# Block-diagonal head product of a linear attention block as three one-pass products of parts

## The chip, the core and the metric

The kernel runs on one core of one Trainium2 chip. The metric is device time in microseconds (us), the median of several executions. Its engines are named as the profile names them: PE is TensorE's matmul, PEld its weight load, DVE VectorE, ACT ScalarE, POOL GpSimd, SP SyncE, which issues nearly all DMAs. Each engine works through its own queue in order; an instruction that waits holds up all that stands behind it on its engine.

## The reference

A linear attention block without softmax, then a two-layer feed-forward block with the gate `h * erf(softplus(h))`:

```python
# q, k, v: (batch 8, heads 8, seq 576, head_dim 64), g_norm: (64,)
kv = np.einsum('bhsd,bhse->bhde', k, v)
out = np.einsum('bhsd,bhde->bhse', q, kv)
rms = np.sqrt(np.mean(out * out, axis=-1, keepdims=True) + 1e-06)
attn = out / rms * g_norm
x = attn.transpose(0, 2, 1, 3).reshape(4608, 512)
h = x @ w_in                                   # (4608, 2048)
sp = np.maximum(h, 0.0) + np.log1p(np.exp(-np.abs(h)))
g = h * erf(sp)
result = g @ w_out                             # (4608, 512)
```

All inputs of the attention are float32; the weights come as float64.

## The kernel before

**Tiles.** The tokens are cut into nine groups of 512: group T = 0 to 7 holds the first 512 positions of batch T, group 8 the last 64 positions of all eight batches. The heads go in pairs, p = 0 to 3. For a pair, two 64x64 products of k and v stand on the diagonal of a 128x128 matrix `bd`; one matmul with `bd` as weights applies both heads to the 128x512 transposed q (line 325, "the product" below). The last 64 positions of the pair go through a small matmul of their own (line 324, the "tail"), and are kept in `x_last` for group 8.

**Number formats.** A matmul on float32 operands is two instructions in the trace; on `float32r` operands it is one. The large products of the later groups are made of float32r parts. `thirds` (line 424) cuts a tensor into `high` (a rounded copy, ACT), `low` (the rest, DVE) and `both` (4096 low + high, DVE); `lower_w` (line 431) does the like for weights. `product` (line 449) then adds up high*high and low*low in the bank `n_ps` and both*both in the bank `m_ps`, and the result is `4095 n_ps + m_ps`: ACT or DVE scales `n_ps` into SBUF, and DVE adds `m_ps` (`add`, line 444).

**Phases.** Groups 0 and 1 and the first attention pairs are worked off by 250 us, with the weights converted, cut into parts and written to DRAM. From there to the end a loop over periods m = 8 to 36 (from line 787) runs groups 2 to 8 and reads the parts of the weights back from DRAM by SP. A period makes four *units* (tiles of 128 columns of h) of a group's first layer, and four *results* (rows of 128 tokens) of the second layer for the four units of the period before; b = m mod 4 is the number of the period within its group. In a period the order in which instructions are issued is, for each of the four units i: 12 matmuls (`hidden`, line 506); for i = 0 ACT's `cut_upper` of both halves of the gated h of the period before; for i = 0 and 1 DVE's `cut_lower` of one half (two 128x1024 operations); ACT's scaling of `n_ps` and DVE's `add` of `m_ps` into h; ACT's softplus. Then two Erf operations on ACT. Then for each of the four results j: 12 matmuls (`result`, line 766), DVE's scaling of `n_ps` (for b = 1, where the sum of a group starts, as a `tensor_scalar` into `es[j]`, line 776; else `add_scaled`), and DVE's `add`. After result 1 DVE multiplies h by the gate (line 876). The matmul products turn through six PSUM banks in pairs.

**The pieces of the attention.** In group T's period b the pair p = b of group T+1 is prepared, as six pieces that `attention` returns: products with loads of later pairs, apply, halve, mean, norm, split. The tuple `places` (line 800) says where each is put: place 0 is ahead of unit 0, place i+1 behind unit i, place 5+j behind result j. So before the change, `products` (k*v, the transposes of q, DVE's copies to `bd`, ACT's copy of `qT`) stands ahead of unit 0, `apply` (tail, product, the copy to `x_last`, ACT's square) behind unit 1, `halve` (DVE splits the squares into two float32r parts) and the loads behind unit 2, `mean` (matmul with a matrix of means, and Ln, Exp and Square on ACT between two table loads) behind result 0, `norm` (three DVE operations) behind result 1, `split` (`thirds` of x) behind result 3. In a group's last period (b = 3) split comes one place earlier.

**Banks and buffers of the attention.** `ps_at` has two banks, for `kv_ps`, `qt_ps`, `se_ps` and `ms_ps` in turn. SBUF tiles with one buffer each carry the tags `qT`, `rms_r`, `sq_lo` and, in pool `x_new`, `x`.

Of the kernel before, what the change touches and what calls it, by code (L numbers as in the profile page):

```python
# [39 lines left out]
FP32 = mybir.dt.float32  # L40
# [14 lines left out]
FIRST = 2  # L55
# [5 lines left out]
def kernel(  # L61
# [207 lines left out]
    def attention(T, p, pools=None):  # L269

        st = {}

        halves = FIRST <= T < B
        bd = bd_kv[:, (T * NP + p) % 2, :]

        q_tail, o_tail = slice(P, 2 * P), slice(2 * P, 2 * P + R)

        def bank(name):
            pool, tag = (pools or {}).get(name, (ps_at, "at"))
            return pool.tile([P, G], FP32, name=name, tag=tag)  # L280

        def square_tile(name):

            if T == 0:
                return gate.tile([P, G], FP32, name=name, tag="h")
            return attp.tile([P, G], FP32, name=name, tag="qT")

        def products():

            kv_ps = st["kv"] = bank("kv_ps")  # L290
            ks, vs, qs = (x.pop((T, p)) for x in (k_sb, v_sb, q_sb))
            C = chunks(T)
            for c in range(C):
                rows = slice(0, S // C + (c < S % C))
                for i in range(2):
                    s = slice(i * D, i * D + D)
                    nc.tensor.matmul(  # L297
                        kv_ps[s, s],
                        lhsT=ks[rows, i, c],
                        rhs=vs[rows, i, c],  # L300
                        start=(c == 0),
                        stop=(c == C - 1),
                    )
            if p % 2 == 0:
                nc.tensor.transpose(kv_ps[:, q_tail], q_last[:, p // 2], ident)
            if p == NP - 2:
                for i in range(NP):
                    load_last(T + 1, i)
            st["qT"] = square_tile("qT")
            for i in range(2):  # L310
                s = slice(i * D, i * D + D)
                nc.vector.tensor_copy(out=bd[s, s], in_=kv_ps[s, s])
            if p % 2 == 0:
                tails[T] = attp.tile([P, P], FP32, name="qT_last", tag="t")
                nc.vector.tensor_copy(out=tails[T], in_=kv_ps[:, q_tail])
            st["tail"] = tails[T][:, p % 2 * R : p % 2 * R + R]
            qt_ps = bank("qt_ps")
            for j in range(J):
                nc.tensor.transpose(qt_ps[:, j * P : j * P + P], qs[:, j], ident)  # L319
            nc.scalar.copy(st["qT"], qt_ps)  # L320

        def apply():
            qT, o_ps, kv_ps = st["qT"], bank("se_ps"), st.pop("kv")
            nc.tensor.matmul(kv_ps[:, o_tail], lhsT=bd, rhs=st.pop("tail"), start=True, stop=True)  # L324
            nc.tensor.matmul(o_ps, lhsT=bd, rhs=qT, start=True, stop=True)  # L325
            nc.vector.tensor_copy(out=x_last[:, p, T * R : T * R + R], in_=kv_ps[:, o_tail])
            st["o"] = o_ps
            nc.scalar.activation(qT, o_ps, AF.Square)

        def square():  # L330
            st["o"], st["qT"] = x_last[:, p, :], square_tile("sq")
            nc.scalar.activation(st["qT"], st["o"], AF.Square)

        def halve():
            sq = st.pop("qT")
            hi = st["hi"] = attp.tile([P, G], FP32R, name="sq_hi", tag="rms_r")
            lo = st["lo"] = attp.tile([P, G], FP32R, name="sq_lo", tag="sq_lo")
            nc.vector.tensor_copy(out=hi, in_=sq)
            nc.vector.tensor_tensor(out=lo, in0=sq, in1=hi.bitcast(FP32), op=ALU.subtract)

        def mean(table=True):
            ms = st["ms"] = bank("ms_ps")
            if halves:


                nc.tensor.matmul(ms, lhsT=mean_w, rhs=st.pop("hi"), start=True, stop=False)  # L346
                nc.tensor.matmul(ms, lhsT=mean_w, rhs=st.pop("lo"), start=False, stop=True)  # L347
                u = square_tile("u")
            else:
                u = st.pop("qT")  # L350
                nc.tensor.matmul(ms, lhsT=mean_w.bitcast(FP32), rhs=u, start=True, stop=True)  # L351
            if T > 0:
                r = attp.tile([P, G], FP32, name="rms_r", tag="rms_r")
                exp_ln_table()
            else:
                r = gate.tile([P, G], FP32, name="rms_r", tag="s")
            st["u"], st["r"] = u, r
            nc.scalar.activation(r, ms, AF.Ln, bias=eps_col)
            nc.scalar.activation(r, r, AF.Exp, scale=-0.5)
            nc.scalar.activation(u, r, AF.Square)  # L360
            if table and (T > 0 or p == NP - 1):
                softplus_table()

        def norm():
            ms, u, r = (st.pop(name) for name in ("ms", "u", "r"))
            nc.vector.scalar_tensor_tensor(
                out=u, in0=ms, scalar=EPS, in1=u, op0=ALU.add, op1=ALU.mult
            )
            nc.vector.scalar_tensor_tensor(
                out=u, in0=u, scalar=3.0, in1=r, op0=ALU.subtract, op1=ALU.mult  # L370
            )
            if T < FIRST:
                if T not in xT:
                    xT[T] = wide.tile([P, KC, G], FP32, name="xT", tag="ab"[T])
                x = xT[T][:, p, :]
            else:
                x = st["x"] = x_new.tile([P, G], FP32, name="x", tag="x")
            nc.vector.scalar_tensor_tensor(
                out=x,
                in0=st.pop("o"),  # L380
                scalar=gm_col,
                in1=u,
                op0=ALU.mult,
                op1=ALU.mult,
            )

        def split():
            if T >= FIRST:
                thirds(st.pop("x"), *(form[:, p] for form in x_forms[T]))

        def loads():
            load_pair(T * NP + p + 2)

        if T == 0:
            return products, apply, halve, mean, norm
        if T == B:
            return lambda: None, square, lambda: None, mean, norm, split

        pieces = ((products,), (apply,), (halve, loads)) if halves else ((products, loads), (apply,), ())
        return (*(partial(chain, *group) for group in pieces), mean, norm, split)  # L400

# [44 lines left out]

    banks = [(ps_h, "h"), (ps_h, "h")] + [(ps_o, f"o{i}") for i in range(4)]

    def product(weights, moving, turns=True):


        n_ps, m_ps = (
            pool.tile([P, G], FP32, name=name, tag=tag)
            for name, (pool, tag) in zip(("n_ps", "m_ps"), banks[:2])
        )
        if turns:
            banks.extend(banks[:2])
            del banks[:2]
        for ps, forms in ((n_ps, (0, 1)), (m_ps, (2,))):
            for k in range(4):  # L460
                for form in forms:
                    nc.tensor.matmul(  # L462
                        ps,
                        lhsT=weights(form, k),
                        rhs=moving(form, k),
                        start=(form == forms[0] and k == 0),
                        stop=(form == forms[-1] and k == 3),
                    )
        return n_ps, m_ps
# [276 lines left out]

    low_room.close()
    room.close()
    ctx.enter_context(tc.tile_pool(name="shift", bufs=1, side="right")).tile([P, 504], FP32, name="shift")
    late_r = ctx.enter_context(tc.tile_pool(name="late_r", bufs=1, side="right"))  # L750
    gate_r = ctx.enter_context(tc.tile_pool(name="gate_r", bufs=1, side="right"))
    w_out_p = ctx.enter_context(tc.tile_pool(name="w_out_p", bufs=7, side="right"))
# [13 lines left out]
    def result(T, b, j, g, w):  # L766

        ps = product(
            lambda form, f: g[j // 2][:, form, f, j % 2 * P : j % 2 * P + P],
            lambda form, f: w[f][:, form],  # L770
        )
        if b == 0:
            if j == 0:
                all_e = wide.tile([P, J, DM], FP32, name="e", tag="a")
                es.update((i, all_e[:, i]) for i in range(J))
            nc.vector.tensor_scalar(
                out=es[j], in0=ps[0], scalar1=SHIFT - 1.0, scalar2=None, op0=ALU.mult
            )
        else:
            add_scaled(es[j], ps[0], SHIFT - 1.0)  # L780
        add(es[j], ps[1])
# [5 lines left out]
    for m in range(first_batch, batches + 1):  # L787
# [21 lines left out]
                todo[5] = partial(chain, todo[5], softplus_table)  # L809
        elif b == NB - 1:  # L810
            places = (0, 2, 3, 5, 6, 7)

        def pieces(place):
            while todo and places[-len(todo)] <= place:
# [101 lines left out]
```

## Time and profile before

| what | value |
|---|---|
| timed runs (3) | median 944.7 us, 944.42 to 946.44 |
| span of the profiled execution | 942.4 us |
| mean granted TensorE clock | 0.999 |
| DMA over the span | 275 GB/s of HBM traffic, read and written |
| ACT table loads, all | 1283 ns each |
| first layer, n_ps matmuls | 896, mean 401 ns, 0.1 us idle before all of them |
| the product (line 325), all 32 pairs | 64 instructions, 34.9 us |

The duration of a matmul in the profile overlaps with that of the next, since they are pipelined: the distance from start to start is what a matmul takes of PE. The distance from the last event of the profile to the timed median is 944.7 - 942.4 = 2.3 us. A bracket behind a line of the timeline is the idle time of that engine ahead of the instruction, with what ended it. Busy time in four periods of the last phase, with the clock, the share of DMA and GB/s at the end of each line:

```profile
351.30:376.10 24.80, 24.80 (x133) 20.05 (x131) 20.01 (x30) 15.86 (x22) 0.00 (x0) 1.00 0.86 291
376.10:400.90 24.80, 24.80 (x136) 20.06 (x133) 20.02 (x29) 15.98 (x22) 0.00 (x0) 1.00 0.90 305
400.90:425.70 24.80, 24.80 (x134) 20.05 (x130) 20.01 (x30) 15.87 (x22) 0.00 (x0) 1.00 0.94 317
425.70:450.50 24.80, 24.80 (x136) 20.06 (x134) 19.98 (x29) 15.99 (x22) 0.00 (x0) 1.00 0.88 305
```

The columns are the stretch, its length, and the busy time of PE, PEld, DVE, ACT and POOL.

### The profile page before, as it was taken

What the parts mean: (1) busy time and instruction counts of PE and PEld (TensorE: products, weight loads), DVE (VectorE), ACT (ScalarE), POOL (GpSimd) and SP (SyncE); (2) the same over time, 40 slices, a digit from 0 to 9 for tenths busy, and PEclk for the clock granted to TensorE, in tenths of its full rate; (3) what the DMA queues carried; (4) which work ended last, traced back from release to release, by engine and by line L of the source; (5) the groups of instructions that cost most, each with busy time, mean ns of one, the idle gap of its engine ahead of it and who ended that gap; (6) DMA issues with size and microseconds to landing.
All of it is one profiled execution on the core that took longest, in us unless ns stands there. A gap on an engine that the chain in (4) does not pass through costs nothing.

```text
span 942.4 us, 11743 instructions
## 1 busy us (share of the span) xinstructions
PE 924.8 (98%) x4272; PEld 683.4 (73%) x4272; DVE 742.6 (79%) x1056; ACT 615.6 (65%) x825; POOL 2.4 (0%) x10
## 2 busy tenths in 40 slices
PE   6999999999999999999999999999999999999997
PEld 4444445666688888888888888888888888888886
DVE  3999858887577787877778888878887877787667
ACT  3899776776766666666666666666666666665551
POOL 1000000000000000000000000000000000000000
PEclk9999999999999999999999999999999999999999
DMA  9766406899699998998899889998896778778871
GB/s 257 276 204 207 150 1 227 318 351 335 214 363 335 309 325 283 306 311 307 280 287 314 294 298 309 311 303 296 293 325 260 263 253 345 284 286 287 353 263 46
DMA packets 111842, 259.78 MB, mean 276 GB/s; under 512 B 43864, under 2 KB 69544, under 8 KB 111784
## 3 DMA queue, kind: packets, MB, share of 16 engines
q1 hardware_dynamic: 110152, 256.73, 78.7%
q10 hardware_dynamic: 1568, 2.29, 0.8%
q8 instruction: 34, 0.56, 0.2%
q14 instruction: 24, 0.20, 0.1%
q0 software_dynamic: 64, 0.00, 0.0%
HBM read 224.40 MB, written 34.60 MB: 275 GB/s over the span
## 4 chain that ended last, share of the span: by engine, by line
PE 92%; DVE 4%; DMA 2%; ACT 1%; issue 0%; SPq 0%; DVEq 0%
PE n_ps L462 45%; PE m_ps L462 22%; PE o_ps L520 10%; PE h_ps L692 6%; PE se_ps L325 3%; PE kv_ps L297 2%; PE qt_ps L319 2%; DMA w_raw<-in_moe_w_in_dram 1%; PE ms_ps L351 1%; DMA v_sb<-in_v_dram 1%; DVE h L876 1%; DVE e L445 1%; PE ms_ps L346 1%; PE ms_ps L347 1%; PE kv_ps L324 1%; DVE e L440 0%
## 5 line engine op out<-in xcount | busy, mean ns | idle before, releaser
L462 PE MATMUL n_ps<-x_forms,w_in_parts 128*128 128x512 f32 x896 | 232.5, 401 | 0.1
L462 PE MATMUL n_ps<-w_out_parts,g_forms 128*128 128x512 f32 x928 | 231.2, 391 | 0.0
L462 PEld LDWEIGHTS n_ps<-w_out_parts,g_forms 128*128 128x128 f32 x928 | 174.2, 188 | 38.4 <-issue 1.4
L462 PEld LDWEIGHTS n_ps<-x_forms,w_in_parts 128*128 128x128 f32 x896 | 166.8, 188 | 43.1 <-issue 9.3
L852 ACT ACTIVATE s<-h 128x512 f32<-128x512 f32 x112 | 71.0, 633 | 178.9 <-DVE h L445 178.9
L445 DVE TENSOR_TENSOR h<-m_ps,h 128x512 f32<-128x512 f32 x116 | 79.7, 687 | 59.8 <-ACT h L837 43.8
L462 PE MATMUL m_ps<-w_out_parts,g_forms 128*128 128x512 f32 x464 | 124.2, 389 | 0.0
L462 PE MATMUL m_ps<-x_forms,w_in_parts 128*128 128x512 f32 x448 | 120.0, 390 | 0.0
L520 PE MATMUL o_ps<-w_out_sb,h_sb 128*128 128x512 f32 x224 | 100.8, 593 | 0.3 <-DVE h_sb L642 0.3
L462 PEld LDWEIGHTS m_ps<-w_out_parts,g_forms 128*128 128x128 f32 x464 | 87.1, 188 | 18.0
L462 PEld LDWEIGHTS m_ps<-x_forms,w_in_parts 128*128 128x128 f32 x448 | 84.1, 188 | 17.7
L445 DVE TENSOR_TENSOR e<-m_ps,e 128x512 f32<-128x512 f32 x116 | 80.2, 692 | 18.2 <-PE m_ps L462 10.9
L440 DVE SCALAR_TENSOR_TENSOR e<-n_ps,e 128x512 f32<-128x512 f32 x88 | 60.3, 685 | 39.2 <-PE n_ps L462 39.2
L520 PEld LDWEIGHTS o_ps<-w_out_sb,h_sb 128*128 128x128 f32 x224 | 42.3, 190 | 48.9 <-issue 46.6
L411 DVE SCALAR_TENSOR_TENSOR g_forms<-g_forms 128x1024 fp32r<-128x1024 f32 x58 | 71.1, 1225 | 2.0
L408 DVE TENSOR_TENSOR g_forms<-h,g_forms 128x1024 fp32r<-128x1024 f32 x58 | 70.6, 1217 | 1.7 <-ACT g_forms L405 1.4
L876 DVE TENSOR_TENSOR h<-h,s 128x1024 f32<-128x1024 f32 x58 | 68.3, 1218 | 0.7 <-ACT s L856 0.7
L837 ACT ACTIVATE h<-n_ps 128x512 f32<-128x512 f32 x112 | 65.5, 585 | 3.4 <-PE n_ps L462 3.4
L405 ACT ACTIVATE g_forms<-h 128x1024 fp32r<-128x1024 f32 x58 | 58.9, 1059 | 12.2 <-PE m_ps L462 8.7
L692 PE MATMUL h_ps<-xT,w_in_sb 128*128 128x512 f32 x144 | 64.9, 594 | 0.7 <-DVE w_in_sb L240 0.6
L106 ACT ACT_TABLE_LOAD x44 | 56.5, 1283 | 0.8
L856 ACT ACTIVATE s<-s 128x1024 f32<-128x1024 f32 x56 | 56.2, 1052 | 0.3
(98 smaller groups left out, 1013.3 us busy)
## 6 DMA issues: line engine op xcount, KB each, us to landing
w_out_parts<-w_out SPq DMA_DIRECT2D x116, 768.0 KB
w_in_parts<-w_in SPq DMA_DIRECT2D x112, 768.0 KB
w_in<-w_new SPq DMA_DIRECT2D x16, 768.0 KB
q_sb<-in_q_dram SPq DMA_DIRECT2D x32, 256.0 KB
w_raw<-in_moe_w_out_dram SPq DMA_DIRECT2D x8, 1024.0 KB
out_dram<-e SPq DMA_DIRECT2D x32, 256.0 KB
k_sb<-in_k_dram SPq DMA_DIRECT2D x28, 287.5 KB
v_sb<-in_v_dram SPq DMA_DIRECT2D x28, 287.5 KB
```

The lines of the kernel that those rows point to most:

```text
L106: nc.scalar.preload_act_table_set("softplus")
L405: nc.scalar.activation(high, x, AF.Copy, scale=1.0 + 2.0**-13)
L408: nc.vector.tensor_tensor(out=low, in0=x, in1=high.bitcast(FP32), op=ALU.subtract)
L411: nc.vector.scalar_tensor_tensor(out=both, in0=low.bitcast(FP32), scalar=SHIFT, in1=high.bitcast(FP32), op0=ALU.mult, op1=ALU.add,)
L440: nc.vector.scalar_tensor_tensor(out=out_, in0=ps, scalar=scale, in1=out_, op0=ALU.mult, op1=ALU.add)
L445: nc.vector.tensor_tensor(out=out_, in0=ps, in1=out_, op=ALU.add)
L462: nc.tensor.matmul(ps, lhsT=weights(form, k), rhs=moving(form, k), start=(form == forms[0] and k == 0), stop=(form == forms[-1] and k == 3),)
L520: nc.tensor.matmul(o_ps[j], lhsT=g[:, j * P : j * P + P], rhs=w_out_sb[:, f, :], start=(f == 0), stop=last,)
L692: nc.tensor.matmul(plain[i], lhsT=w_in_sb[:, c, i % FC * P : i % FC * P + P], rhs=xT[T][:, c, :], start=(c == 0), stop=(c == KC - 1),)
L837: nc.scalar.activation(h[:, i], n_ps, AF.Copy, scale=SHIFT - 1.0)
L852: nc.scalar.activation(s[:, i], h[:, i], AF.Softplus)
L876: nc.vector.tensor_tensor(out=part(h, half), in0=part(h, half), in1=part(s, half), op=ALU.mult)
```

## The change

For groups T = 3 to 7 and pairs p = 0 to 2, fifteen pairs in all (`parts` in the diff), the float32 product on `bd` becomes three float32r matmuls on parts: `kv` holds the three parts of `bd`, formed on DVE behind the copies to `bd`; `q3` holds the three parts of the transposed q, `high` taken by ACT from PSUM in place of the copy to `qT`, and `low` and `both` by DVE in a new piece, `cut`. `apply_parts` issues the tail, the three matmuls into the next pair of the six large banks, ACT's scaling of `n_ps` into `o`, DVE's add of `m_ps`, and ACT's square. Such a pair has seven pieces, at the places 0, 2, 3, 4, 6, 7, 8: products ahead of unit 0, cut behind unit 1, apply behind unit 2, halve and loads behind unit 3, mean behind result 1, norm behind result 2, split behind result 3. Some tiles take other buffers. The other pairs keep their pieces and places.

For all groups of the last phase, the scaling of the first `n_ps` of a result (b = 1) goes from DVE to ACT. A pool of 504 floats per partition that only shifted what follows gives way to one of 384 for `kv`.

```diff
@@ attention
+        parts = FIRST < T < B and p < NP - 1
@@ products
-            st["qT"] = square_tile("qT")
+            if not parts:
+                st["qT"] = square_tile("qT")
             for i in range(2):
                 s = slice(i * D, i * D + D)
                 nc.vector.tensor_copy(out=bd[s, s], in_=kv_ps[s, s])
+            if parts:
+                kv = st["kv3"] = parts_p.tile([P, 3, P], FP32R, name="kv_forms", tag="kv3")
+                nc.vector.tensor_scalar(
+                    out=kv[:, 0],
+                    in0=bd,
+                    scalar1=(1.0 + 2.0**-13) / SHIFT,
+                    scalar2=None,
+                    op0=ALU.mult,
+                )
+                lower_w(bd, *(kv[:, i] for i in range(3)))
...
-            nc.scalar.copy(st["qT"], qt_ps)
+            if parts:
+                x = st["q3"] = [
+                    pool.tile([P, G], FP32R, name=f"q_{name}", tag=tag)
+                    for name, pool, tag in (
+                        ("high", attp, "rms_r"),
+                        ("low", attp, "sq_lo"),
+                        ("both", x_new, "x"),
+                    )
+                ]
+                upper(qt_ps, x[0])
+                st["qt"] = qt_ps
+            else:
+                nc.scalar.copy(st["qT"], qt_ps)
+
+        def cut():
+            lower(st.pop("qt"), *st["q3"])
+
+        def apply_parts():
+            x, w, kv_ps = st.pop("q3"), st.pop("kv3"), st.pop("kv")
+            nc.tensor.matmul(kv_ps[:, o_tail], lhsT=bd, rhs=st.pop("tail"), start=True, stop=True)
+            n_ps, m_ps = two_banks()
+            for i, ps in enumerate((n_ps, n_ps, m_ps)):
+                nc.tensor.matmul(ps, lhsT=w[:, i], rhs=x[i], start=(i != 1), stop=(i != 0))
+            nc.vector.tensor_copy(out=x_last[:, p, T * R : T * R + R], in_=kv_ps[:, o_tail])
+            o = st["o"] = attp.tile([P, G], FP32, name="o", tag="qT")
+            nc.scalar.activation(o, n_ps, AF.Copy, scale=SHIFT - 1.0)
+            add(o, m_ps)
+            st["qT"] = x_new.tile([P, G], FP32, name="sq", tag="x")
+            nc.scalar.activation(st["qT"], o, AF.Square)
@@ mean
-                u = square_tile("u")
+                u = (
+                    x_new.tile([P, G], FP32, name="u", tag="x")
+                    if parts
+                    else square_tile("u")
+                )
@@ norm
+            elif parts:
+                x = st["x"] = u
@@ end of attention
+        if parts:
+            return products, cut, apply, partial(chain, halve, loads), mean, norm, split
@@ product: its choice of banks becomes a function, which apply_parts calls too
+    def two_banks(turns=True):
+        ps = [
+            pool.tile([P, G], FP32, name=name, tag=tag)
+            for name, (pool, tag) in zip(("n_ps", "m_ps"), banks[:2])
+        ]
         if turns:
             banks.extend(banks[:2])
             del banks[:2]
+        return ps
@@ pools of the last phase
-    ctx.enter_context(tc.tile_pool(name="shift", bufs=1, side="right")).tile([P, 504], FP32, name="shift")
+    parts_p = ctx.enter_context(tc.tile_pool(name="parts_p", bufs=1, side="right"))
@@ result
-            nc.vector.tensor_scalar(
-                out=es[j], in0=ps[0], scalar1=SHIFT - 1.0, scalar2=None, op0=ALU.mult
-            )
+            nc.scalar.activation(es[j], ps[0], AF.Copy, scale=SHIFT - 1.0)
@@ loop over periods
+        if len(todo) > len(places):
+            places = (0, 2, 3, 4, 6, 7, 8)
```

More of the change, by code (lines that the diff above doesn't have):

```diff
@@ L319, in products @@
                 nc.tensor.transpose(qt_ps[:, j * P : j * P + P], qs[:, j], ident)
-            nc.scalar.copy(st["qT"], qt_ps)
+            if parts:
[25 more added lines that the diff above has]
+            nc.scalar.activation(st["qT"], o, AF.Square)
         def apply():
+            if parts:
+                return apply_parts()
             qT, o_ps, kv_ps = st["qT"], bank("se_ps"), st.pop("kv")
@@ L397, in attention @@
             return lambda: None, square, lambda: None, mean, norm, split
+        if parts:
+            return products, cut, apply, partial(chain, halve, loads), mean, norm, split
         pieces = ((products,), (apply,), (halve, loads)) if halves else ((products, loads), (apply,), ())
@@ L447 @@
     banks = [(ps_h, "h"), (ps_h, "h")] + [(ps_o, f"o{i}") for i in range(4)]
-    def product(weights, moving, turns=True):
-        n_ps, m_ps = (
+    def two_banks(turns=True):
+        ps = [
             pool.tile([P, G], FP32, name=name, tag=tag)
             for name, (pool, tag) in zip(("n_ps", "m_ps"), banks[:2])
-        )
+        ]
         if turns:
@@ L458, in product @@
             del banks[:2]
+        return ps
+    def product(weights, moving, turns=True):
+        n_ps, m_ps = two_banks(turns)
         for ps, forms in ((n_ps, (0, 1)), (m_ps, (2,))):
@@ L775, in result @@
                 es.update((i, all_e[:, i]) for i in range(J))
-            nc.vector.tensor_scalar(
-                out=es[j], in0=ps[0], scalar1=SHIFT - 1.0, scalar2=None, op0=ALU.mult
-            )
+            nc.scalar.activation(es[j], ps[0], AF.Copy, scale=SHIFT - 1.0)
         else:
```

## The prediction

> **What bounds the kernel now.** I read the page's busy shares and chain of waits first, then the groups by form for the product that is replaced, then the timeline of PE, DVE and ACT one at a time over four periods of the last phase (one period is four units of the first layer and four results of the second, 24.78 us on average: the same PE place falls at 352.51 and, four periods on, at 451.63). Busy shares and chain:
>
> ```profile
> PE 924.8 (98%) x4272; PEld 683.4 (73%) x4272; DVE 742.6 (79%) x1056; ACT 615.6 (65%) x825; POOL 2.4 (0%) x10
> ...
> PE 92%; DVE 4%; DMA 2%; ACT 1%; issue 0%; SPq 0%; DVEq 0%
> ```
>
> PE is back to back, and the chain that ended last is PE itself. So PE time saved in a period is time gained, as long as PE never waits; and a wait put before PE costs its whole length. The average share of 79% on DVE hides the question: when in a period is DVE free? Groups by form, then PE and DVE over one period (start us, duration us, then the work):
>
> ```profile
> L325 PE MATMUL se_ps<-qT,bd_kv 128*128 128x512 f32 x64 | 34.9, 628 | 0.0
> ```
>
> ```profile
> 418.97 1.07 PE L462 MATMUL m_ps<-w_out_parts,g_forms 128*128 128x512 f32 x4
> ...
> 431.20 1.08 PE L462 MATMUL m_ps<-x_forms,w_in_parts 128*128 128x512 f32 x4
> 432.12 0.33 PE L324 MATMUL kv_ps<-qT_last,bd_kv 128*128 128x64 f32 x2
> 432.29 1.08 PE L325 MATMUL se_ps<-qT,bd_kv 128*128 128x512 f32 x2
> ...
> 435.04 1.07 PE L462 MATMUL m_ps<-x_forms,w_in_parts 128*128 128x512 f32 x4
> ```
>
> ```profile
> 420.08 0.69 DVE L445 TENSOR_TENSOR e<-m_ps,e 128x512 f32<-128x512 f32 x1 [0.22 <-PE m_ps L462]
> 420.69 2.35 DVE L876 TENSOR_TENSOR h<-h,s 128x1024 f32<-128x1024 f32 x2
> 422.96 0.68 DVE L366 SCALAR_TENSOR_TENSOR u<-ms_ps,u 128x512 f32<-128x512 f32 x1
> ...
> 427.85 0.68 DVE L408 TENSOR_TENSOR x_forms<-x,x_forms 128x512 fp32r<-128x512 f32 x1
> 428.57 0.69 DVE L411 SCALAR_TENSOR_TENSOR x_forms<-x_forms 128x512 fp32r<-128x512 f32 x1
> 429.18 0.45 DVE L312 COPY bd_kv<-kv_ps 64x64 f32<-64x64 f32 x2
> 429.66 1.22 DVE L408 TENSOR_TENSOR g_forms<-h,g_forms 128x1024 fp32r<-128x1024 f32 x1
> ...
> 432.18 0.69 DVE L445 TENSOR_TENSOR h<-m_ps,h 128x512 f32<-128x512 f32 x1
> ...
> 435.18 0.68 DVE L445 TENSOR_TENSOR h<-m_ps,h 128x512 f32<-128x512 f32 x1
> 435.78 0.21 DVE L326 COPY x_last<-kv_ps 128x64 f32<-128x64 f32 x1
> 437.53 0.69 DVE L445 TENSOR_TENSOR h<-m_ps,h 128x512 f32<-128x512 f32 x1 [1.54 <-ACT h L837]
> ```
>
> The bracket is the idle time before an instruction. DVE waits for PE at result 1 (420.08), and from there it works without a gap until 435.98: all its free time of the period (1.54 here, and 0.6, 0.2, 1.6 and 0.2 at results 0 and 1) lies later. Call R1 the moment when PE ends result 1: 418.97 plus four matmuls at 0.2265 (1.81 from the first of eight to the ninth) = 419.88. DVE is through "add h of unit 1" at 435.78, R1+15.9. PE meanwhile reaches the end of unit 2 at 435.95 with the old product in it.
>
> [...] the m_ps of units 1 and 2 start 3.84 apart, those of units 2 and 3 2.72, so tail and product take 1.12, two instructions of about 0.43 being the product. [...] 0.69 us for a 128x512 subtraction, 0.42 for the cast of the same shape. [...] the moved copies should add no table load; the trace shows copies (L837, L405) beside softplus without a load, none directly after Erf.
>
> **The product on PE, 15 times.** Removed: 0.86. Added: three one-pass matmuls at the 0.2265 spacing of L462 = 0.68. Saved 0.18 each, 2.7 us in all, if nothing waits. The tail matmul stays.
>
> **DVE, added before the product, in queue order.** At place 0, behind the two bd copies, three 128x128 operations form the parts of the weights. Nearest rows: 0.21 from start to start for the qT_last copy, 0.227 for the 128x128 cast[...]; each depends on the one before, which costs 0.03 (L408 to L411: 0.72 from start to start for 0.69). Bounds 0.63 to 0.96, taken 0.87. At place 2, behind add h of unit 1, the cut: the L408 and L411 pair on 128x512, 1.33 from start to start (427.85 to 429.18), 1.41 to the end of the write. So from R1: 15.9 + 0.87 + 1.41 = R1+18.18. Even pairs copy qT_last too (0.21): R1+18.39. The norm now stands behind result 2 and the mean behind result 1, but these only change places within the gapless stretch; its sum stays.
>
> **PE, at the same place.** From R1: the moved mean 0.47, results 2 and 3 5.44, products and transposes 1.36 (425.32 to 426.68 by the same reckoning), units 0 to 2 8.16: it arrives at R1+15.43. Tail and first matmul run (0.45), then PE waits for low and at last for both, until R1+18.24 with 0.06 for the semaphore (ACT starts 0.03 after DVE in the softplus rows). Third matmul 0.23, then unit 3, results 0 and 1 (8.16): the next R1 is 26.63 after the last, for odd pairs; 26.84 for even ones. Against 24.78 that is +1.85 and +2.06. The 0.18 saved lies inside this wait and is worth nothing. Behind the waiting matmul in PE's queue stands unit 3, and everything after it.
>
> Does DVE recover before the next R1? Add h of unit 2 ends at 18.8, softplus, the new ACT copy of o (0.58), add o (DVE, 0.69) until 20.7, Square, copy of h, add h of unit 3 until 22.5, halves until 23.6; result 0 is read by 24.9, and result 1's n_ps comes only at 25.95. About 1 us of room: yes, each period starts afresh. PSUM has room: six banks in three pairs, nine pairs a period now; unit 3 takes unit 1's pair, free at 16.8, before the cut.
>
> **The scaling of results, DVE to ACT, in the periods with b = 1.** It takes 4 x 0.61 from DVE, but puts 4 x 0.58 into ACT's queue, which at that place is:
>
> ```profile
> 391.23 1.28 ACT L856 ACT_TABLE_LOAD   x1
> 392.52 2.01 ACT L856 ACTIVATE s<-s 128x1024 f32<-128x1024 f32 x2
> 394.55 1.28 ACT L103 ACT_TABLE_LOAD   x1
> ...
> 397.88 1.28 ACT L106 ACT_TABLE_LOAD   x1
> ```
>
> With pair 1 (next R1 at 26.63): softplus of unit 3 ends at 23.2, table 24.5, Erf 26.5, copies of results 0 and 1 27.6; then the mean's table, Ln, Exp, Square and table (4.6 us: 394.55 to 399.16 in the trace) 32.25; copy of result 2 32.85. DVE waits for each: add of result 1 ends 28.4 (R1+1.8, otherwise 0.8), gates R1+4.05, add of result 2 R1+6.9, norm 8.95, add of result 3 9.55, where the unmoved order has 7.97. So pair 2, which follows, starts 1.6 later: 26.84 + 1.64 = 28.48, +3.7. Bounds: 0, if DVE's saved 2.4 covered the waits, to 2.5, if the ACT backlog delays the following cut_upper too. The same edit without parts, at 770.5 to 793: there the mean stands behind result 0, so result 1's copy is behind the whole 4.6 us, its add ends 5 us after R1 instead of 0.8, and DVE enters the next period about 4 late; unit 3 there needs unit 0's banks, whose add then ends at about 805.4, where PE would begin its m_ps at 803.1: +2.5 (0 to 4). At 873 to 882 no mean stands in ACT's queue, and the adds end as before: 0.
>
> **Other edits.** A fourth pair (p = 3) has no parts, but carries the mean of pair 2: +0.47. In the first such period (from 253) DVE still waits 0.72 for ACT ahead of the g_forms: there the wait costs 1.0, not 2.06. The pair's loads go one place later; they fetch two periods ahead, some 50 us, and the queue that they are moved behind is one w_out load: 0. If that cover were gone, kv_ps would wait for v_sb, as it does only in the first stage now. The new SBUF pool is 480 bytes smaller than the one that it replaces: nothing in the trace prices it, 0.
>
> **Sum.** Per four pairs 2.06 + 1.85 + 3.7 + 0.47 = 8.08; five times 40.4; less 1.06 for the first; plus 2.5: +41.8. On the profiled span of 942.4 that is 984.2; the median of the timed runs lies 2.3 above the span: 986.5, +4.4%.
>
> **Rivals.**
> 1. The product pays as meant: 942.4 - 2.7 + 2.3 = 942.0, faster by 0.3%. For it: PE is the bound and its work falls. Against: 2.3 us of DVE work would have to fit between R1 and the product, where the trace has no gap. It holds if the cut ended before PE comes to the second matmul, 15.43 + 0.45 = R1+15.9; each 0.1 later costs 0.1 per pair.
> 2. The wait comes, but the move to ACT is free (DVE's saving covers it): 986.5 - 5 x 1.64 - 2.5 = 976. For it: ACT has 35% free on the average. Against: the order of its queue.
> 3. DVE doesn't recover: the chain of add, softplus, copy, add in units 2 and 3 with the o steps between uses up the 1 us of room, and lateness is handed to the next period. At 1 us in each of 15 periods: 1001. For it: ACT waits 179 us for DVE's h before softplus today. Against: the room just counted.
> 4. A change too small to tell (below 0.2%, about what this measurement can tell): it needs an exact balance.
>
> **Numbers.** Forecast 0.62, rival 1 0.05, rival 2 0.13, rival 3 0.18, rival 4 0.02. Range: the weights' parts at 0.63 and rival 2 give 986.5 - 3.6 - 10.7 = 972; some lower for a smaller cut; rival 3 with parts at 0.96 gives 1002. Taken 968 to 1002. Faster 0.05, same 0.02, slower 0.93.
>
> **What would show it.** Right: PE (or its weight load) waits on the DVE line of both_only, some 2 us, 15 times, nearly 4 after pairs 1; three matmuls at 0.23 in place of 0.86; DVE busy without a gap from result 1 to the cut. Wrong: no PE wait before the product (then rival 1); equal waits in pairs 1 and 2 (rival 2); DVE without idle time at results 0 and 1 (rival 3).

## The result, and the profile after

The changed kernel takes 996.5 us (median of four runs, 994.2 to 997.2) against 944.6 us for the one before on the same chip: a ratio of 1.0544, with an interval of 1.0529 to 1.0559. The profiled execution spans 995.0 us, 52.6 more than before, at a mean granted clock of 0.988 instead of 0.999. Forecast were 986.5 us in a range of 968 to 1002: the direction and most of the size are right, the time is 10 us too low.

The page's busy times and the engines' shares of the chain that ended last:

```profile
PE 945.9 (95%) x4287; PEld 692.9 (70%) x4287; DVE 763.3 (77%) x1118; ACT 639.5 (64%) x868; POOL 2.4 (0%) x10
...
PE 64%; DVE 19%; ACT 8%; issue 5%; DMA 3%; SPq 1%; DVEq 0%; ACTq 0%
```

The span grew by 52.6 us and PE's busy time by 21.1, although the program gives PE less to do. The first says that PE now waits (DVE and ACT take 27% of a chain that was 92% PE), the second that PE's own work takes longer, because it is slower or because its matmuls overlap less. What PE waits for, largest entries of the view of waits on PE (total us, times, longest us):

```profile
PE n_ps L354 <- DVE q_low L459: 26.3, 15, 2.5
PE kv_ps L298 <- DMA v_sb<-in_v_dram: 7.4, 3, 5.8
PE m_ps L354 <- DVE q_both L462: 3.4, 15, 0.2
```

The middle line belongs to the phases ahead of 250 us, and the kernel before has it too (8.9 us in four waits). The other two are the new product, 15 times each: 29.7 us. One of them in PE's timeline, the product of a first pair (start us, duration us, work, idle time ahead and its releaser):

```profile
367.78 1.10 PE L517 MATMUL m_ps<-x_forms,w_in_parts 128*128 128x512 f32 x4
368.72 0.33 PE L351 MATMUL kv_ps<-qT_last,bd_kv 128*128 128x64 f32 x2
368.85 0.48 PE L354 MATMUL n_ps<-q_high,kv_forms 128*128 128x512 f32 x1
371.07 0.50 PE L354 MATMUL n_ps<-q_low,kv_forms 128*128 128x512 f32 x1 [1.73 <-DVE q_low L459]
371.79 0.50 PE L354 MATMUL m_ps<-q_both,kv_forms 128*128 128x512 f32 x1 [0.23 <-DVE q_both L462]
```

DVE at the same place, and below it the three new operations at the place of the products, some 19 us later:

```profile
369.73 0.68 DVE L496 TENSOR_TENSOR h<-m_ps,h 128x512 f32<-128x512 f32 x1
370.33 0.68 DVE L459 TENSOR_TENSOR q_low<-qt_ps,q_high 128x512 fp32r<-128x512 f32 x1
371.05 0.69 DVE L462 SCALAR_TENSOR_TENSOR q_both<-q_low,q_high 128x512 fp32r<-128x512 f32 x1
...
390.18 0.23 DVE L317 TENSOR_SCALAR kv_forms<-bd_kv 128x128 fp32r<-128x128 f32 x1
390.44 0.29 DVE L483 SCALAR_TENSOR_TENSOR kv_forms<-kv_forms,bd_kv 128x128 fp32r<-128x128 f32 x1
390.77 0.29 DVE L486 TENSOR_TENSOR kv_forms<-kv_forms 128x128 fp32r<-128x128 f32 x1
```

PE comes to the second matmul at 369.34 and gets it at 371.07, when DVE, which had no gap, has written `q_low` (at 371.01, 0.06 us earlier). Afterwards the unit goes on. So the wait that was forecast is there, at the forecast place. It costs a little more than its bracket says: the first and second matmul start 2.22 us apart, where undisturbed ones of this product start 0.24 apart (shown below, under `late_dve_pad`), so 1.98 us are lost, not 1.73. At 0.25 in each of 30 waits that is an estimated 7.5 us, and it stands in PE's busy time.

To see where the rest lies, take the distance from unit 0's `m_ps` in one period to the same in the next, and add up four periods (three pairs with parts and one without). The excess over the kernel before, in us, by stages of four periods; the last two columns are experiments that are told below:

| stage (first pair with parts, start) | forecast | after | fill_wait | es_on_dve |
|---|---|---|---|---|
| 1 (T = 3, from 253) | 7.0 | 8.2 | 7.0 | 5.1 |
| 2 (T = 4) | 8.1 | 8.4 | 8.3 | 6.9 |
| 3 (T = 5) | 8.1 | 9.6 | 8.1 | 6.6 |
| 4 (T = 6) | 8.1 | 9.9 | 8.3 | 6.8 |
| 5 (T = 7) | 8.1 | 12.6 | 8.1 | 6.6 |
| 6 (no parts, only the scaling on ACT) | 2.5 | 3.9 | 3.9 | 1.3 |
| 7 (no parts) | 0 | 0.2 | 0.2 | 0.2 |
| sum | 41.8 | 52.8 | 43.9 | 33.4 |

The sum is 52.8 and not the 52.6 of the spans, because the changed kernel is 0.2 us ahead when stage 1 starts. In stage 2 the forecast holds within 0.3 us; stages 1, 3, 4 and 5 have something else, in steps of about 1.5. It is the clock. The view of windows on six stretches (columns: stretch, length, busy time of PE, PEld, DVE, ACT and POOL, then granted clock, DMA share, GB/s), with an undisturbed stretch in the second row:

```profile
319.24:322.65 3.41, 3.41 (x10) 2.64 (x9) 0.69 (x1) 1.79 (x4) 0.00 (x0) 0.50 0.96 251
322.65:326.06 3.41, 3.41 (x17) 2.77 (x16) 2.71 (x5) 2.25 (x3) 0.00 (x0) 1.00 1.04 341
479.66:483.07 3.41, 3.41 (x10) 2.64 (x9) 1.00 (x3) 1.75 (x3) 0.00 (x0) 0.50 0.83 212
588.89:592.30 3.41, 3.41 (x10) 2.65 (x9) 0.69 (x1) 2.08 (x4) 0.00 (x0) 0.50 0.81 223
698.12:701.53 3.41, 3.41 (x9) 2.63 (x8) 0.69 (x1) 1.92 (x4) 0.00 (x0) 0.50 0.90 237
725.42:728.83 3.41, 3.41 (x8) 2.74 (x9) 1.33 (x3) 1.75 (x3) 0.00 (x0) 0.50 0.76 242
756.14:759.55 3.41, 3.41 (x9) 2.65 (x8) 0.69 (x1) 1.93 (x4) 0.00 (x0) 0.50 0.54 227
```

In each of the six PE runs 8 to 10 matmuls where it otherwise runs 17. The periods that contain them are 1.35 to 1.6 us longer than their undisturbed likes (29.4 against 27.8 for a third pair, 28.8 against 27.3 for a first or second one): 9.1 us together. The kernel before has no such stretch between 15 and 939 us, so its profile could not show the term.

### The profile page after: what moved, and what is told of

The parts are those of the page before. It is cut to its first block, busy times and chain, and to the rows that moved or that the text cites. A ratio compares the mean times of both kernels' runs of the same rounds, so it can differ in the third digit from the quotient of the medians.

```text
span 995.0 us, 11946 instructions
## 1 busy us (share of the span) xinstructions
PE 945.9 (95%) x4287; PEld 692.9 (70%) x4287; DVE 763.3 (77%) x1118; ACT 639.5 (64%) x868; POOL 2.4 (0%) x10
## 3 DMA queue, kind: packets, MB, share of 16 engines
q10 hardware_dynamic: 1568, 2.29, 0.8%
## 4 chain that ended last, share of the span: by engine, by line
PE 64%; DVE 19%; ACT 8%; issue 5%; DMA 3%; SPq 1%; DVEq 0%; ACTq 0%
PE n_ps L517 30%; PE m_ps L517 14%; PE o_ps L575 9%; PE h_ps L747 5%; DVE g_forms L459 3%; DVE h L496 3%; DVE e L496 2%; PE kv_ps L298 1%; ACT s L911 1%; DVE h L931 1%; PE se_ps L367 1%; PE qt_ps L331 1%; DMA k_sb<-in_k_dram 1%; DMA w_raw<-in_moe_w_in_dram 1%; ACT L103 1%
## 5 line engine op out<-in xcount | busy, mean ns | idle before, releaser
L517 PE MATMUL n_ps<-x_forms,w_in_parts 128*128 128x512 f32 x896 | 235.7, 406 | 1.1 <-DVE e L491 0.6
L517 PEld LDWEIGHTS n_ps<-x_forms,w_in_parts 128*128 128x128 f32 x896 | 171.0, 193 | 41.4 <-issue 2.4
L517 PE MATMUL m_ps<-x_forms,w_in_parts 128*128 128x512 f32 x448 | 123.7, 399 | 0.8 <-DVE e L496 0.8
L517 PEld LDWEIGHTS m_ps<-x_forms,w_in_parts 128*128 128x128 f32 x448 | 86.4, 193 | 20.9 <-DVE e L496 1.2
```

The lines of the kernel that those rows point to most:

```text
L517: nc.tensor.matmul(ps, lhsT=weights(form, k), rhs=moving(form, k), start=(form == forms[0] and k == 0), stop=(form == forms[-1] and k == 3),)
```

## The experiments

All kernels compute the same values; they differ in the order of the work, in the engine that does it or in padding, or they repeat work. Times are medians, with the ratio to the kernel before.

**Scaling of the results back on DVE** (`es_on_dve`), to tell the queue of ACT from the rest:

```diff
-            nc.scalar.activation(es[j], ps[0], AF.Copy, scale=SHIFT - 1.0)
+            nc.vector.tensor_scalar(
+                out=es[j], in0=ps[0], scalar1=SHIFT - 1.0, scalar2=None, op0=ALU.mult
+            )
```

> The changed kernel with the scaling of the first result banks (b = 1) back on DVE; all else as changed. Theory of the queue order on ACT: the wait ahead of the product in pair 2 falls by 1.6 us to that of pair 0, five times, the stretch of group 8's preparation gets back 2.5 us, and with shorter waits one or more of the drops of the granted clock go: 996.5 - 8.2 - 2.5 - 1.5 to 4.5 = 981 to 984. Rival, DVE's work counts by its sum: 4 x 0.61 us more on DVE in each of these periods lengthens them: 997 to 1008.

Measured: 979.3 us, 1.0379 (1.0352 to 1.0407), 17.2 less than after and somewhat better than expected. The queue of ACT that costs this, in the changed kernel's timeline at a second pair:

```profile
404.82 2.01 ACT L911 ACTIVATE s<-s 128x1024 f32<-128x1024 f32 x2
406.74 1.07 ACT L831 ACTIVATE e<-n_ps 128x512 f32<-128x512 f32 x2
407.82 1.28 ACT L103 ACT_TABLE_LOAD   x1
409.12 0.69 ACT L404 ACTIVATE rms_r<-ms_ps,eps_col 128x512 f32<-128x512 f32 x1
409.84 0.63 ACT L405 ACTIVATE rms_r<-rms_r 128x512 f32<-128x512 f32 x1
410.50 0.63 ACT L406 ACTIVATE u<-rms_r 128x512 f32<-128x512 f32 x1
411.15 1.28 ACT L106 ACT_TABLE_LOAD   x1
412.45 1.08 ACT L831 ACTIVATE e<-n_ps 128x512 f32<-128x512 f32 x2
```

The copies of results 2 and 3 stand behind the mean's logarithm and its two table loads, and DVE's queue behind the copies:

```profile
413.08 0.69 DVE L496 TENSOR_TENSOR e<-m_ps,e 128x512 f32<-128x512 f32 x1 [2.18 <-ACT e L831]
```

Between the profiled executions the difference is 19.0 (995.0 and 976.0), of two kinds. No period of this one has a halved clock, which gives about 9; the rest is the queue. The table's last two columns are both free of halved stretches, and they differ by 1.5 a stage (2.0 in the first, of which 0.4 is fill_wait's own, and 2.6 in stage 6); forecast were 1.64 and 2.5. That this kernel has no halved stretch is partly luck, as is shown below: of its four runs the one with a clock of 0.991 took 985.3 us, those with 0.998 and 0.999 took 977.7 to 979.7.

**The same move alone, in the kernel before** (`es_alone`): the diff above, the other way, in before.

> The kernel before with one part of the change alone: the scaling of the first result banks (b = 1) on ACT instead of DVE. Theory of the order in ACT's queue: result 1's copy stands behind the table loads and functions of the mean, DVE's multiplications and norm come some 3.8 us later, and PE waits some 3 us for the bank of the product (read last by norm) ahead of the next pair's k*v, five times, 2.5 us once more for group 8's preparation, with drops of the clock on top: 960 to 972. Rival, DVE is relieved by 2.4 us in each of these periods and ACT has room: 941 to 946.

Measured: 977.0, 1.0344 (1.0319 to 1.0368), slower than expected. The move hits another place: PE waits for the bank of the mean, which DVE's late norm frees, in five periods.

```profile
409.44 1.33 PE L297 MATMUL kv_ps<-v_sb,k_sb 116*64 116x64 f32 x20 [3.26 <-DVE u L366]
...
411.72 3.65 PE L462 MATMUL n_ps<-x_forms,w_in_parts 128*128 128x512 f32 x8
```

Eight matmuls at 3.65 instead of 1.98 to 2.1: the halved clock again, after another wait and without any of the new operations. So neither the product nor the cut is needed to slow PE; its idle time is the suspect. And the costs of the two parts of the change can't simply be added: with the parts the norm stands behind result 2, here behind result 1, where the same backlog of ACT costs 5.1 to 6.3 us a stage, the clock included.

**The pool's lost 480 bytes given back** (`pad504`):

```diff
     parts_p = ctx.enter_context(tc.tile_pool(name="parts_p", bufs=1, side="right"))
+    parts_p.tile([P, 504 - 3 * P], FP32, name="pad", tag="pad")
```

> The changed kernel with the pool that holds the weights' parts padded to the 504 floats of the pool that it replaced, so that all later SBUF pools lie where they lay before. Theory that addresses set the pitch of the matmuls: the first layer's matmuls of the odd groups go from 0.233 us from start to start back to 0.2265; most of it lies inside the waits ahead of the product, 0.35 us in each of the four periods of group 7 and some 0.1 to 0.2 in the others come out: 993 to 995. Rival, the pitch comes from something else (a clock, DMA traffic): pitch and time unchanged, 996.5.

Measured: 997.1, 1.0549 (1.0534 to 1.0563), no gain in the sum, against an expected 1.5 to 3.5 us. But the addresses do matter: in stages 2, 4 and 6 after has its first-layer matmuls at 0.2337 us each instead of 0.2265 (1.87 instead of 1.81 from a unit's `n_ps` to its `m_ps`), and with the pad all are at 0.2265: periods without parts 24.83 instead of 25.04, the first of stage 6 22.66 instead of 23.00. This run lost it again to the clock: five halved stretches, of which three are 6.8 long.

**The same kernel without and with the pad, in a version whose product doesn't wait** (`late_dve` against `late_dve_pad`, which is told below), to see the pool's price without that noise.

> As late_dve_pad without the padding. Theory that the addresses behind the pool set the pitch of the first layer's matmuls in the odd groups (0.2337 instead of 0.2265 us): without waits for the clock to hide it, 0.35 us in each of the four periods of group 7 and the unpaired periods of groups 3 and 5 show, more where PE binds: 955.5 to 958. Rival, no effect of addresses on time: 954.

Measured: 955.8, 1.0119 (1.0104 to 1.0135), against 954.0 with the pad: 1.8 us, in the periods of stage 6 (23.0 against 22.7), in the unpaired ones of stages 2 and 4 (25.03 against 24.84) and in stage 7.

**The cut one place earlier** (`cut_early`), to see whether the product's wait is the whole of the rest:

```diff
-            places = (0, 2, 3, 4, 6, 7, 8)
+            places = (0, 1, 3, 4, 6, 7, 8)
```

> The changed kernel with the cut of q one place earlier, behind unit 0 and so ahead of DVE's cut of the second half of h and the add of unit 1; the same work on every engine. Theory of the order in DVE's queue: the cut ends 3.0 us earlier, at R1+15.2, before PE comes for it at R1+15.9; no wait in pairs 0 and 1, some 1 us in pair 2 (behind the results scaled on ACT), no drop of the granted clock: 948 to 958. Rival, DVE's sum of work binds and the wait only moves (to a bank of unit 3 or of result 0, or to the parts of h): 975 to 996.

Measured: 989.8, 1.0483 (1.0468 to 1.0497): a miss by 30 us. The product's wait is nearly gone (0.9 us in all), and the first pair's period is 24.55, below the 24.72 of before. But most of that is lost at other places of PE's timeline:

```profile
397.43 1.20 PE L517 MATMUL m_ps<-x_forms,w_in_parts 128*128 128x512 f32 x4 [0.63 <-DVE h L496]
...
411.20 0.33 PE L306 MATMUL kv_ps<-ident,q_last 128*128 128x128 f32 x1
414.57 0.93 PE L331 MATMUL qt_ps<-ident,q_sb 128*128 128x128 f32 x4 [3.04 <-DVE u L412]
415.15 3.51 PE L517 MATMUL n_ps<-x_forms,w_in_parts 128*128 128x512 f32 x8
```

Unit 3 waits for unit 1's banks, whose add now stands behind the cut. And when PE isn't held up at the product, it comes to the next transposes before the norm has freed their bank, 16.2 us in ten waits, with the halved clock behind some (3.51 for eight). The norm is late because of the scaling on ACT. The wait at the product had covered this one: of two waits in series the later one was hidden.

**Early cut, scaling on DVE, and the pad together** (`all_three`):

> The changed kernel with the cut behind unit 0, the scaling back on DVE and the pool padded. Theory that the long wait with the early cut came from the scaling on ACT (norm late, so that the transposes of q wait for the bank of the mean): that wait goes, and what is left is unit 3's wait for the bank of unit 1, some 0.6 us in each of the fifteen pairs: 946 to 955. Rival, DVE's work binds by its sum: 965 to 980.

Measured: 972.6, 1.0292 (1.0277 to 1.0307). This is in the range of the rival. The wait for the transposes falls to 0.2 and the clock stays at 0.998, but unit 3's `m_ps` waits 0.65 for DVE in 14 periods and, apart from the first (24.55), a pair's period stays at 26.3 to 26.9. Once PE gets through the product early, DVE is late at the next place: an earlier cut moves the wait, and the 2.3 us of new DVE work stay in the same stretch.

**The cut where it was, the product one unit later** (`late_dve_pad`): scaling on DVE, the pad, and

```diff
-            places = (0, 2, 3, 4, 6, 7, 8)
+            places = (0, 2, 4, 5, 6, 7, 8)
```

> The changed kernel with the product one unit later still (apply behind unit 3, halves behind result 0; the cut stays behind unit 1), the scaling back on DVE and the pool padded. Theory of the order in DVE's queue: PE comes for the low part at R1+15.4+2.7+0.4 = R1+18.6, when DVE has it (R1+17.5, both at 18.2 to 18.4): no wait ahead of the product, no drop of the clock, and PE's saving of 15 x 0.18 shows: 941 to 945. Rival, DVE's sum of work binds wherever the product stands: the wait moves to a bank, the mean or the transposes, 955 to 975.

Measured: 954.0, 1.0094 (1.0079 to 1.0109): missed by 9, though the product waits no more. The lateness appears at the mean, whose squares DVE splits after result 0:

```profile
365.14 0.40 PE L354 MATMUL n_ps<-q_low,kv_forms 128*128 128x512 f32 x1
365.38 0.40 PE L354 MATMUL m_ps<-q_both,kv_forms 128*128 128x512 f32 x1
...
371.39 0.47 PE L388 MATMUL ms_ps<-sq_hi,mean_w 128*128 128x512 f32 x1 [0.17 <-DVE sq_hi L380]
372.02 0.50 PE L389 MATMUL ms_ps<-sq_lo,mean_w 128*128 128x512 f32 x1 [0.16 <-DVE sq_lo L381]
```

From the third pair on, a pair's period takes 25.4 to 25.55: with the same work on DVE as in `es_on_dve`, the later place of the product and of what follows it brings the excess of a pair down from 2.0 to 2.6 us to some 0.7. Here one sees the product itself unhindered, at 0.24 from start to start.

**The same with the parts of the weights on GpSimd** (`late_pool`): `nc.vector` becomes `nc.gpsimd` in the three operations, which are four there.

> As late_dve_pad, with the weights' parts formed on GpSimd, which is idle in this phase, in four 128x128 operations instead of DVE's three. Theory: with the product late, DVE's chain through a whole period sets the end (the halves come 0.7 us after PE wants them for the mean); 0.83 us less on DVE takes that wait away in each of the fifteen pairs: 941 to 945, so the 2.7 us saved on PE may just show. Rival: GpSimd is slow or disturbs DVE, or the ACT chain of unit 3 and o sets the halves: 951 to 960.

Measured: 945.6 (21 runs) against 944.4 (25 runs of before), 1.0012 (1.0006 to 1.0019). This is just outside the expected 941 to 945. The three operations, some 0.8 us a pair, are gone from DVE, and the periods fall to 24.55 to 25.07. GpSimd has time for it, but DVE works slower beside it. First GpSimd's timeline, then DVE's:

```profile
354.80 0.53 POOL L317 TENSOR_SCALAR kv_forms<-bd_kv 128x128 fp32r<-128x128 f32 x1 [46.13 <-PE m_ps L524]
355.41 1.15 POOL L325 TENSOR_SCALAR kv_forms<-kv_forms 128x128 fp32r<-128x128 f32 x1
356.64 1.10 POOL L328 TENSOR_TENSOR kv_forms<-kv_forms,bd_kv 128x128 fp32r<-128x128 f32 x1
357.82 0.46 POOL L329 TENSOR_TENSOR kv_forms<-kv_forms 128x128 fp32r<-128x128 f32 x1
```

```profile
354.88 1.29 DVE L466 TENSOR_TENSOR g_forms<-h,g_forms 128x1024 fp32r<-128x1024 f32 x1
...
357.94 1.42 DVE L466 TENSOR_TENSOR g_forms<-h,g_forms 128x1024 fp32r<-128x1024 f32 x1
```

These take 1.22 alone. So DVE's busy time falls by only 7.44 us in all (from 779.97 in `late_dve_pad` to 772.53), about 0.5 a pair. With all this moved, the new product is 0.12% behind the old one. In the profile the weight load of the mean still waits for `sq_lo`, 5.9 us in 14 periods, against the 2.7 us that the product saves on PE; how much of the 5.9 PE itself loses was not separated. No version that was run beats the kernel before.

**PE kept busy during the wait** (`keep_busy`), to test whether its idle time is what halves the clock: the first of the three matmuls is repeated five times, which gives the same sum in the bank.

```diff
             for i, ps in enumerate((n_ps, n_ps, m_ps)):
+                for n in range(5 if i == 0 else 0):
+                    nc.tensor.matmul(ps, lhsT=w[:, i], rhs=x[i], start=True, stop=True)
```

> The changed kernel with the first of the three matmuls of the product given out six times instead of once (each writes the same values anew), so that PE idles 1.1 us less in each wait; DVE's and ACT's work is the same. Theory that the granted clock drops because PE idles: the clock stays at 1.00, the matmuls behind the waits keep 0.2265 us, and six drops of about 1.5 us go: 986 to 990. Rival, the drop has another cause: the clock falls as before and the time stays at 996 or rises by the added matmuls in the first pair, whose wait is short (to 998).

Measured: 989.9, 1.0475 (1.0460 to 1.0489): five more matmuls a pair make the kernel 6.7 us faster. Its profile has two halved stretches where that of after has six, both in third pairs, though their wait is only 1.31 + 0.23.

That did not fit a limit on the length of a wait. In after itself a wait of 1.40 was followed by a halved stretch, and waits of 2.29 and 2.48 were not. The starts of the halved stretches, worked out from the clock in windows of 1 us, answer it: in after they lie 47, 32, 32, 8 and 9 times 3.413 us apart, each within 0.02 us, and in the other kernels too the distances are whole multiples; every stretch inside the last phase is 3.41 or 6.83 long. So in these profiles the halved stretches lie on a fixed grid of 3.413 us: 436.90 us from the first start in after to the sixth (319.24 to 756.14, above) are 128 steps. Counted is PE's idle time in each window of the grid that was at full clock, from 250 us to the last 10 us, over six kernels (after, pad504, keep_busy, es_alone, cut_early, es_on_dve):

| idle in one window | windows | followed by a halved one |
|---|---|---|
| 0.80 to 1.50 us | 52 | 0 |
| 1.54 to 1.74 us | 5 | 3 |
| 1.78 to 3.26 us | 19 | 19 |

In a window that was itself halved, less idle time was enough: after 0.43 us or more the next was halved too in six of six cases, after 0.40 us or less in none of 22. That is where the stretches of 6.83 us come from.

**More repeats where the wait is longer** (`fill_wait`): 7, 5 and 9 in place of five, in the first, second and third pair of a group, so that no window is idle for 1.5 us.

> The after kernel with 7, 5 and 9 repeats of the first of the three matmuls in the first, second and third pair of a group (keep_busy had 5 in each), so that PE's idle time ahead of the second matmul falls from 2.5 to about 0.5 us while the wait for VectorE's cut stays where it is. Theory of windows: PE's clock is halved for 3.41 us when more than about 1.5 us of one 3.41 us window of a fixed grid were idle; no window has that much any more, so no halved stretch is left in the pairs, all third pairs take about 27.8 (keep_busy had 29.4 in two of five), the span is about 985 to 986, the median 986 to 988. Rival, the halving comes from something else at that place (the cut, the three products, a transfer) and not from PE's idle time: one or more periods of 29 again, span 988 to 990, as in keep_busy.

Measured: 988.3, 1.0463 (1.0449 to 1.0478), span 986.8, clock 1.000: no halved stretch is left, and all five third pairs take 27.8, as expected. Span and median are a little above the expected ones: 0.4 of it is the very first pair's period, 26.16 instead of 25.73 in keep_busy, as its repeats are longer than its wait; the rest lies ahead of the last phase. The waits are filled:

```profile
PE m_ps L356 <- DVE q_both L464: 3.2, 14, 0.2
PE n_ps L356 <- DVE q_low L461: 2.8, 10, 0.4
```

This settles the rest of the excess: PE does useless work in the place of its wait, the period is still set by DVE, and what has changed is the clock afterwards.

## Why the prediction was right, and where it was not

- *DVE gapless from result 1 to the cut, so a wait before the product.* Shown, with its size. In es_on_dve, where neither ACT's queue nor the clock is in it, the distances from result 1 to result 1, as the forecast counts, are in stage 3 longer than before by 2.04, 1.99, 2.07 and 0.47 for the pairs 0 to 3. Forecast, without the move to ACT, were 2.06, 1.85, 2.06 and 0.47. (The table counts from unit 0, where the 0.47 of the mean falls to the first pair.) The discount of the very first pair was too small: 1.06 were forecast, and in the table's count it came at 1.01 where later first pairs came at 2.5, which is 1.5 less. The three operations on the weights add 0.81 ahead of the `g_forms`: 390.98 - 389.69, less the 0.48 of the copies. The 0.87 forecast was the author's estimate; no row of before has a two-tensor operation on 128x128. In the changed kernel each of the two takes 0.29 (at 390.44 and 390.77).
- *The scaling on ACT delays the third pair and stage 6.* Shown in size: 1.5 a stage against 1.64 (the forecast's own figures, 9.55 less 7.97, give 1.58), and 2.6 in stage 6 against 2.5 (where 805.4 less 803.1 would be 2.3). In a third pair the place is right too: from result 1 to result 1 it is 3.57 above before in stage 3 of fill_wait, and 3.7 were forecast. In stage 6 the place is not: one wait of unit 3 for unit 0's banks was forecast, and in the changed kernel three shorter ones stand, of unit 0 and unit 1 for the results of the period before, and of unit 1 once more a period later. That the sum agrees there is luck. No table load was added for the copies: there are 113 before and after, and in the queue above the copies at 406.74 follow Erf (404.82) with none between, and those at 412.45 follow the mean's second. Rival 2, the move for free, is out: the first pair's wait of 1.73 becomes 2.29 in the third, while without the move it is 1.26. The three waits of stage 6 in PE's timeline, with the lines between them left out:

```profile
842.75 2.12 PE L517 MATMUL n_ps<-x_forms,w_in_parts 128*128 128x512 f32 x8 [0.37 <-ACT e L831]
...
848.46 1.20 PE L517 MATMUL m_ps<-x_forms,w_in_parts 128*128 128x512 f32 x4 [0.78 <-DVE e L496]
...
870.50 2.14 PE L517 MATMUL n_ps<-x_forms,w_in_parts 128*128 128x512 f32 x8 [0.63 <-DVE e L491]
```

- *DVE recovers before the next result 1.* Shown in stages 2 to 5: without the clock each stage costs 8.1 to 8.3, and lateness is not handed on through the period without parts (24.85 in stages 1 and 3, against 24.84 before). Rival 3 gives nearly the measured time, and is wrong all the same: its 15 us were to be spread over all fifteen pairs, and the time that the forecast lacks lies in six of them, in the clock.
- *PE saves 0.18 a pair and gets nothing of it.* Shown from the other side: where nothing waits, in the first pair of cut_early and of late_pool, the period is 24.55 instead of 24.72.
- *The price of the new SBUF pool, 0.* This step failed. "Nothing in the trace prices it" was true, but 0 wasn't the only answer. It is 1.9 us: 0.2 in each of two periods without parts, 1.3 in stage 6, 0.2 in stage 7. The two runs with and without the pad say 1.8.
- *The sum.* It treated a wait of PE as costing its own length, and so missed the term that makes most of the error: six windows of half clock, 9.1 us. "A wait put before PE costs its whole length" is the sentence that was wrong. What the profiles show of this term is stretches of 3.41 us at a granted clock of 0.50, behind windows in which PE idled: in the six kernels counted, 1.54 to 1.74 us in one window halved the clock in three cases of five, and 1.78 us or more in all 19.

41.8 forecast, 1.9 for the pool and 9.1 for the clock make 52.8, which is the sum of the stages. That it agrees to a tenth is luck: single terms are off by 0.1 to 0.7 us either way.

## What to carry to other kernels

When PE, having never waited, is made to wait, price the wait twice: its length, and what it does to the granted clock afterwards; here a wait of about 2 us cost 1.5 us more in 6 of 15 cases. A gain on the engine that bounds the kernel is only worth what the others' order leaves free at that place, and removing one wait shows the one that stood behind it, so reckon the slack of all places of the period before moving a piece. A pool's size is part of a change, since what lies behind it shifts; here 480 bytes per partition less cost 1.8 us (late_dve against late_dve_pad).

## What was not expected of the hardware

- The granted clock of PE fell to 0.50 for whole windows of a 3.413 us grid, after idle time of PE in the window before: none of 52 at 0.80 to 1.50 us, all 19 from 1.78 in the six kernels counted, where the window before was at full clock. In the last microseconds of fill_wait, which is not among them, a window with 1.84 us idle was followed by one at full clock, so the limit is not sharp. The grid's phase isn't the kernel's (from the first `m_ps` of stage 1 its next edge lies 2.9 us away in after, 0.45 in pad504, 2.2 in before), which fits waits that are hit in one run and not in the next: after ran from 994.2 to 997.2 at mean clocks of 0.988 to 0.993, es_on_dve from 977.7 to 985.3 at 0.999 to 0.991, while fill_wait, whose windows up to there are never that idle, stayed between 987.3 and 988.6 at 0.998 to 1.000.
- Matmuls of the same shape took 0.2337 us from start to start in after (stages 2, 4 and 6) and 0.2265 in pad504, by the address of their tiles: the two kernels differ in a shift of 480 bytes per partition alone. Why is open; no shift but this one was tried.
- DVE's 128x1024 subtraction took 1.29 and 1.42 us beside GpSimd's work instead of 1.22, which took back part of what the move gave.
- Why two windows of 1.67 and 1.74 us idle were not followed by half clock, and two of 1.54 were, stays open.
